# Joining 64-bit weights with a shift, equal halves of the query projection, and a list of the order written anew

## The chip, the cores and the metric

The kernel runs on one core of a Trainium2 chip. The metric is the device time of one execution in microseconds (us). The core's engines are named as in the profile: PE (TensorE) multiplies matrices, DVE (VectorE), ACT (ScalarE) and POOL (GpSimd) work element by element, and SP (SyncE) issues the transfers that the DMA engines carry out. SBUF is the core's working memory, PSUM the memory into which PE writes.

## The reference

A linear attention with exponential features feeds a feed-forward block with a squared ReLU:

```python
def phi(x):                      # x is q or k: (8, 8, 576, 64); w_phi: (64, 128)
    proj = np.einsum('bhsd,df->bhsf', x, w_phi)
    proj = proj - np.max(np.abs(proj), axis=-1, keepdims=True)
    return np.concatenate([np.exp(proj), np.exp(-proj)], axis=-1)
q_p, k_p = (phi(q), phi(k))
kv = np.einsum('bhsf,bhsd->bhfd', k_p, v)
z = np.sum(k_p, axis=2)
num = np.einsum('bhsf,bhfd->bhsd', q_p, kv)
den = np.einsum('bhsf,bhf->bhs', q_p, z)[..., None] + 1e-06
x = (num / den)                  # rearranged to (4608 tokens, 512)
h = x @ w_in                     # (512, 2048)
r = np.maximum(h, 0.0)
out = (r * r) @ w_out            # (2048, 512)
```

The two weight matrices arrive as 64-bit floats; q, k, v and w_phi are 32-bit.

## The kernel before

The attention works on 32 pairs of heads (8 batches of 8 heads). The first six pairs (`early`) get their denominators by extra matmuls; the other 26 (`late`, `visit`) do it by transposes and sums on DVE. In `visit` PE does the keys of one pair, the key-value product of the pair before and the numerators of the one before that, one behind another. In `late` the query projection (`q_proj`, L894) is done in four matmuls per pair: 512 columns for each of two heads into the PSUM tile pp, and the other 64 of each into pn and pv; three copies bring them to the SBUF tile pt, and POOL reduces pt over its partitions (L907).

The early pairs send their denominators through memory: a copy on ACT into sx, a DMA to den (L745), a reciprocal on DVE (L754, L755), a DMA to the scratch rd (L758) and one that spreads rd to rb (L765). DVE then multiplies the numerators n by rb (L772). The late pairs send the key-value block through a scratch too: td from kvs (L859), and eight transfers from td to kz (L864).

The feed-forward block takes 18 chunks of 256 tokens. A chunk has 8 steps, one for each slice of 256 hidden units. A step is a first product (`gemm1`, L973: 24 matmuls from the halves of the weights, win, and of the tokens, ring), then r, gh and ph on ACT and gl on DVE, and a second product (`gemm2`, L1000: 12 matmuls). The second product has three kinds of operands: gh with the high part wh, gh with the low part and gl with the near part. For slices 0 to 5 the low and near parts are bf16 tiles (wl); for slices 6 and 7 they are every second bf16 of float32r tiles (wout). Behind the last step of a chunk DVE scales the two PSUM banks po into the tile o, of which there is one buffer (L1011), and SP stores them (L1014).

Each of the 16 weight slices (8 of w_in, 8 of w_out, 1024 KB each) has to be joined from two 32-bit words to a 32-bit float. `prep` loads a slice into raw; ACT scales the high word into u (L435) and turns the low word into rounding bits (L440); DVE puts sign and rounding bits together (L443) and joins them with the shifted u (L447). A w_in slice then takes its maximum on ACT (L464); `power` spreads it over the partitions by a matmul (L389) and works out a scale on DVE (L393 to L397), and the scaled slice is split into win on ACT (L468) and DVE (L470). A w_out slice goes to its high part on ACT (L488), the low part on POOL (L300) and the near part on DVE (L495). Several slices lie in turn in the same SBUF space (home_of).

The order of all instructions is written by a planner. Every operation (`P.add`) has an engine, a duration, what it waits for and a rank; the planner runs a clock of its own and, on each engine, takes the ready operation of lowest rank. The ranks stand in a table of characters (RANKS). On the chip each engine and SP work strictly in the order so written.

Of the kernel before, what the change touches and what calls it, by code (L numbers as in the profile page):

```python
# [18 lines left out]
U32 = mybir.dt.uint32  # L19
AF = mybir.ActivationFunctionType  # L20
# [33 lines left out]
COLD = 1.15  # L54
# [9 lines left out]
class Op:  # L64
    __slots__ = ("n", "ways", "eng", "fn", "after", "uses", "rank", "land", "mode", "start", "end", "left", "next")

    def __init__(self, n, ways, after, uses, rank, land, mode):
        self.n, self.ways, self.rank, self.land, self.mode = n, ways, rank, land, mode
        self.take(next(iter(ways)))
        self.after, self.uses = [a for a in after if a is not None], list(uses)  # L70
        self.start = self.end = None

# [4 lines left out]
class Plan:  # L77
# [16 lines left out]
    def add(self, eng, us, fn, after=(), uses=(), rank=0.0, land=0.0, mode=WHOLE, lock=None, other=None):  # L94
        ways = {eng: (us, fn, lock)}
        if other:
            ways[other[0]] = other[1:]
        op = Op(len(self.ops), ways, after, uses, rank, land, mode if isinstance(mode, tuple) else (mode, mode))
        self.ops.append(op)
        return op  # L100

    def close(self):
# [6 lines left out]
        for (tag, n), mine in users.items():  # L109
            first = mine[0]  # L110
            if tag in self.single:
                if last := users.get((tag, (n[0], n[1] - 1))):
                    first.after += last[:1]
            else:
                if old := users.get((tag, n - self.bufs[tag])):
                    first.after += old
                if last := users.get((tag, n - 1)):
                    first.after.append(last[0])
            for op in mine[1:]:
                op.after.append(first)  # L120
# [28 lines left out]
    def order(self):  # L149
        for op in self.ops:  # L150
            op.start = op.end = None
            op.next, op.left = [], 0
            op.after = [a for a in {id(a): a for a in op.after}.values() if a is not op]
        for op in self.ops:
            for a in op.after:
# [6 lines left out]
        mode = WHOLE  # L162
# [6 lines left out]
        def release(op):  # L169
            least = max([open_at.get(tag, 0.0) for tag, n in alone(op)], default=0.0)  # L170
            for eng in op.ways:
                at = least
                for a in op.after:
                    at = max(at, a.end + a.land + (self.HOP[a.eng] if a.eng != eng or a.land else 0.0))
# [10 lines left out]
        while done < len(self.ops):  # L185
# [39 lines left out]
            free[e] = op.end  # L225
# [61 lines left out]
def tile_kernel(ctx, tc, qp, kp, vp, w_phi, w_in, w_out, out):  # L287
# [28 lines left out]
    wout = [None] * NFP  # L316
# [33 lines left out]
    td_ = tiles(dr, "td", [128, 256], F32, 2, EARLY)  # L350
    rb_ = tiles(at, "rb", [128, S], F32, 2)
    vm_ = tiles(sm, "vm", [128, NP], F32, 2)
    pw_ = tiles(sm, "pw", [128, 2], F32, 2)
# [11 lines left out]
    o_ = tiles(mp, "o", [128, DM], F32, 1)  # L365
# [9 lines left out]
    ld_w = P.add("SP", 1.5, lambda: SP.dma_start(wraw, w_phi), [], [], -100.0, land=2.0)  # L375
# [7 lines left out]
    def power(src, dst, top, after, uses, rank):  # L383
        n = power_n[0]
        power_n[0] += 1
        key = [("pw", n)] + uses

        def gather():
            PE.matmul(out=pn_["pw", n][:, 0:128], lhsT=src().to_broadcast([128, 128]), rhs=ident, start=True, stop=True)  # L389

        def bits():
            p = pw_[n]
            V.tensor_reduce(out=p[:, 0:1], in_=pn_["pw", n][:, 0:128], op=ALU.max, axis=AX.X)  # L393
            V.tensor_scalar(out=p[:, 1:2].bitcast(I32), in0=p[:, 0:1].bitcast(I32), scalar1=0x7F800000,
                            scalar2=None, op0=ALU.bitwise_and)
            V.tensor_scalar(out=dst[:, 0:1], in0=p[:, 1:2], scalar1=TINY, scalar2=top, op0=ALU.max, op1=ALU.mult)
            V.reciprocal(out=dst[:, 1:2], in_=dst[:, 0:1])  # L397

        a = P.add("PE", 0.3, gather, after, key + [("pn", ("pw", n))], rank)
        return P.add("DVE", 0.86, bits, [a], key + [("pn", ("pw", n))], rank)  # L400


# [9 lines left out]
    final = lambda f: f"h{f // 2} l{f // 2}".split() if f < NFP - 2 else [home_of[f, False]]  # L412

    def prep(n, f, of_in, rank):
# [3 lines left out]
        box = []  # L418
        raw = lambda: box[0]
        low_w, high_w = (lambda i=i: raw().rearrange("p (c w) -> p c w", w=2)[:, :, i] for i in range(2))  # L420
        u = lambda: u_[0][n]

        def load():
            box.append(cp.tile([128, 2048], I32, name=f"raw{f}{'io'[not of_in]}", tag=home))
            if of_in:
                SP.dma_start(raw().rearrange("p (t c) -> p t c", t=KT),
                             w_in[:, 512 * f:512 * f + 512].rearrange("(t p) c -> p t c", p=128))
            else:
                SP.dma_start(raw().rearrange("p (t c) -> p t c", t=2),
                             w_out[256 * f:256 * f + 256, :].rearrange("(t p) c -> p t c", p=128))  # L430

        def size():
            A.activation(out=u().bitcast(F32), in_=high_w().bitcast(F32), func=AF.Abs, scale=2.0 ** -111)  # L435

        def low():
            A.activation(out=low_w(), in_=low_w().bitcast(U32), func=AF.Copy, scale=0.875 * 2.0 ** -29, bias=0.4995)  # L440

        def ends():
            V.scalar_tensor_tensor(out=low_w(), in0=high_w(), scalar=word(0x80000000), in1=low_w(),  # L443
                                   op0=ALU.bitwise_and, op1=ALU.bitwise_or)
# [5 lines left out]
        def value(t):  # L450
            return u().bitcast(F32).rearrange("p (t c) -> p t c", t=t)

        ld = P.add("SP", 2.7, load, [home_read[home]] if home in home_read else [], [], rank - 3.0 + 0.3 * n, land=2.0)
        l = P.add("ACT", 1.14, low, [ld], [], rank)
        l = P.add("DVE", 1.22, ends, [l], [], rank, lock=4.0)
        o = P.add("ACT", 1.14, size, [ld], key, rank)
        o = P.add("DVE", 1.22, join, [o, l], key, rank, lock=4.0)
        if of_in:
            cs = slice(256 * f, 256 * f + 256)
            m = cw[:, f, :]  # L460
            pm = sm.tile([128, 1], F32, name=f"wm_{f}")

            def most():
                A.activation(out=raw()[:, 0:1024].bitcast(F32), in_=u().bitcast(F32), func=AF.Abs, accum_out=pm)  # L464

            o = home_read[home] = P.add("ACT", 1.06, most, [o], key, rank)
            o = power(lambda: pm, m, TOP_W, [o], [], rank)
            o = P.add("ACT", 1.1, lambda: A.activation(out=win[0][:, :, cs], in_=value(KT), func=AF.Copy, scale=m[:, 1:2]),  # L468
                      [o], key, rank)
            o = P.add("DVE", 1.5, lambda: V.scalar_tensor_tensor(  # L470
                out=win[1][:, :, cs], in0=value(KT), scalar=m[:, 1:2], in1=win[0][:, :, cs], op0=ALU.mult,
                op1=ALU.subtract), [o], key, rank, lock=4.0)
        else:
            home_read[home] = o
            j = slice(2 * (f % 2), 2 * (f % 2) + 2)

            def high():
                if f >= NFP - 2:
                    whole = cp.tile([128, 4, DM], F32R, name=f"wout{f}", tag=home)
                    wout[f] = whole[:, 0:2], whole[:, 2:4]  # L480
                else:
                    if f % 2 == 0:
                        both[f], both[f + 1] = [(
                            cp.tile([128, 4, DM], F32R, name=f"wh{f}", tag=final(f)[0]),
                            cp.tile([128, 8, DM], BF16, name=f"wl{f}", tag=final(f)[1]))] * 2
                    h, l = both[f]
                    wout[f] = h[:, j], l[:, j], l[:, slice(j.start + 4, j.stop + 4)]
                A.activation(out=wout[f][0], in_=value(2), func=AF.Copy)  # L488

            o = P.add("ACT", 1.1, high, [o] + [home_read[x] for x in final(f)], key, rank)  # L490
            last = [P.add("POOL", 2.5, lambda: sub(G, wout[f][1], value(2), wout[f][0].bitcast(F32)),
                          [o], key, rank, lock=0.0)]
            pool_prep.append(last[0])
            if f < NFP - 2:
                last.append(P.add("DVE", 0.75, lambda: V.tensor_copy(out=wout[f][2], in_=value(2)), [o], key, rank, lock=0.6,  # L495
                                  other=("ACT", 1.06, lambda: A.activation(out=wout[f][2], in_=value(2), func=AF.Copy), None)))
            return last
        return [o]

    both = {}  # L500
# [5 lines left out]
    def load_v(p, rank):  # L506
        v_load[p] = P.add("SP", 0.85, lambda: SP.dma_start(v_[p], vp[p]), [], [("v", p)], rank, land=2.0)
# [33 lines left out]
    def loads(p, rank):  # L541
        k_load[p] = P.add("SP", 0.75, lambda: SP.dma_start(k_[p], kp[p]), [], [("k", p)], rank, land=2.0)
# [577 lines left out]
```

## Time and profile before

| | us |
|---|---|
| median of 3 runs | 1072.16 |
| lowest, highest | 1069.67, 1072.84 |
| the profiled execution: its own time | 1070.77 |
| the profiled execution: span from the first to the last instruction | 1068.7 |

The profile's times count from the first instruction of one execution. The mean granted clock of PE was 0.989 of full speed. A busy engine is one on which an instruction was running; idle time is put down to what ended it.

### The profile page before, as it was taken

How to read it: one execution, taken by the hardware profiler on the slowest of the kernel's cores; microseconds unless marked ns; L12 is line 12 of the kernel's file. 1: busy time of each engine (PE TensorE's matmuls, PEld its weight loads, DVE VectorE, ACT ScalarE, POOL GpSimd, SP SyncE). 2: the span in 40 equal slices, each digit the busy share in tenths (PEclk: the TensorE clock that was granted, in tenths of full speed). 3: DMA queues.
4: the chain of work that ended last, by engine and by line, in shares of the span. 5: the costliest groups of instructions: out<-in, count | busy, mean ns of one | idle time of the engine just before them, and what ended most of it. 6: DMA issues, size and time to landing. Idle time of an engine off the chain costs nothing.

```text
span 1068.7 us, 19712 instructions
## 1 busy us (share of the span) xinstructions
PE 1037.3 (97%) x7762; PEld 706.9 (66%) x7762; DVE 740.5 (69%) x1561; ACT 635.1 (59%) x1129; POOL 135.3 (13%) x66
## 2 busy tenths in 40 slices
PE   7878999999999999999999999999999999999997
PEld 5545666676766666676666666666666666777774
DVE  6688898896879787778678768887887854112111
ACT  7888966756666565656455666656556545333232
POOL 0003122102020111111011111111110111000000
PEclk9898999999999999999999999999999999999999
DMA  9743322221222121212112112222121101000000
GB/s 348 257 147 102 132 82 70 72 66 49 70 72 63 44 60 52 76 57 76 57 44 72 46 48 56 77 56 77 44 63 24 51 13 41 1 20 20 2 20 20
DMA packets 68288, 73.48 MB, mean 69 GB/s; under 512 B 36836, under 2 KB 41828, under 8 KB 68196
## 3 DMA queue, kind: packets, MB, share of 16 engines
q1 hardware_dynamic: 68196, 72.23, 21.8%
q8 instruction: 61, 1.00, 0.4%
q14 instruction: 31, 0.25, 0.1%
HBM read 59.18 MB, written 12.99 MB: 68 GB/s over the span
## 4 chain that ended last, share of the span: by engine, by line
PE 86%; ACT 5%; DMA 4%; DVE 3%; SPq 2%; issue 1%; DVEq 0%; ACTq 0%
PE po L1000 35%; PE ph L973 33%; PE pv L606 4%; PE pp L550 2%; PE pn L824 2%; PE pp L894 2%; PE pv L824 2%; DMA den<-sx 1%; SPq L864 1%; PE pv L611 1%; PE pn L556 1%; DMA raw3i<-in_w_in_dram 1%; DMA out_dram<-o 1%; DMA k<-in_kp_dram 1%; DMA td<-kvs 1%
## 5 line engine op out<-in xcount | busy, mean ns | idle before, releaser
L973 PE MATMUL ph<-ring,win 128*128 128x256 f16 x3456 | 397.9, 273 | 1.3 <-DVE gl L300 1.3
L973 PEld LDWEIGHTS <-win 128*128 128x128 f16 x3456 | 335.8, 98 | 65.6 <-issue 5.5
L982 ACT ACTIVATE r<-ph,cw 128x512 f32<-128x512 f32 x144 | 98.8, 686 | 222.9 <-PE ph L973 222.3
L300 DVE TENSOR_TENSOR gl<-ph,gh 128x512 bf16<-128x512 f32 x144 | 98.9, 686 | 168.7 <-ACT ph L986 166.2
L907 POOL PARTITION_ALL_REDUCE mx<-pt x52 | 114.5, 2201 | 626.2 <-ACT pt L304 473.9
L1000 PE MATMUL po<-wh,gh 128*128 128x512 f32 x432 | 129.8, 421 | 2.6 <-DVE o L1011 2.5
L1000 PE MATMUL po<-wl,gh 128*128 128x512 bf16 x432 | 112.1, 382 | 0.0
L1000 PE MATMUL po<-wl,gl 128*128 128x512 bf16 x432 | 110.9, 379 | 0.0
L1000 PEld LDWEIGHTS <-gl 128*128 128x128 bf16 x576 | 56.1, 97 | 69.6
L984 ACT ACTIVATE gh<-r 128x512 fp32r<-128x512 f32 x144 | 90.7, 630 | 6.6 <-PE po L1000 2.3
L1000 PEld LDWEIGHTS <-gh 128*128 128x128 bf16 x576 | 44.8, 98 | 74.1 <-issue 39.5
L1000 PEld LDWEIGHTS po<-wh,gh 128*128 128x128 f32 x432 | 74.0, 189 | 22.3 <-issue 4.4
L986 ACT ACTIVATE ph<-r 128x512 f32<-128x512 f32 x144 | 84.1, 584 | 0.3
L1000 PE MATMUL po<-wout,gh 128*128 128x512 f32 (+1 forms) x288 | 76.1, 405 | 0.0
L606 PE MATMUL pv<-e,v 128*64 128x256 f32 x512 | 62.2, 386 | 0.0
L572 ACT ACTIVATE e<-e 128x512 f32<-128x512 f32 x64 | 39.8, 621 | 31.4 <-DVE e L569 31.2
L300 DVE TENSOR_TENSOR qe<-pt,mx 128x576 f32<-128x576 f32 x52 | 39.1, 753 | 26.9 <-POOL mx L907 26.7
L304 ACT ACTIVATE n<-pn 128x320 f32<-128x320 f32 (+1 forms) x32 | 13.8, 430 | 72.2 <-PE pn L824 70.1
L921 DVE SCALAR_TENSOR_TENSOR pt<-qe,zc,pt 128x576 f32<-128x576 f32 x52 | 41.9, 813 | 12.7 <-ACT pt L919 12.1
L912 ACT ACTIVATE qe<-qe 128x576 f32<-128x576 f32 x52 | 35.0, 673 | 25.1 <-DVE qe L300 25.1
L606 PEld LDWEIGHTS pv<-e,v 128*64 128x64 f32 x512 | 36.2, 140 | 16.4 <-issue 2.5
L1011 DVE TENSOR_SCALAR o<-po,cc 128x512 f32<-128x512 f32 x36 | 28.7, 798 | 25.4 <-DMA out_dram<-o 19.2
(207 smaller groups left out, 1380.1 us busy)
## 6 DMA issues: line engine op xcount, KB each, us to landing
v<-in_vp_dram SPq DMA_DIRECT2D x32, 320.0 KB
k<-in_kp_dram SPq DMA_DIRECT2D x32, 288.0 KB
q<-in_qp_dram SPq DMA_DIRECT2D x32, 288.0 KB
rb<-rd SPq DMA_DIRECT2D x64, 144.0 KB
out_dram<-o SPq DMA_DIRECT2D x36, 256.0 KB
td<-kvs SPq DMA_DIRECT2D x26, 128.0 KB
kz<-td SPq DMA_DIRECT2D x208, 16.0 KB
raw0i<-in_w_in_dram SPq DMA_DIRECT2D x1, 1024.0 KB
```

The source lines that it names most:

```text
L300: eng.tensor_tensor(out=out_, in0=a, in1=b_, op=ALU.subtract)
L572: o = P.add("ACT", act_us(512), lambda n=n: A.activation(out=e_[n][:, :, 1, :], in_=e_[n][:, :, 0, :], func=AF.Exp, scale=-1.0), [o], [("e ...
L606: PE.matmul(out=to[64 * h:64 * h + 64, 0:256], lhsT=v_[p][:, t, h, :], rhs=e_[2 * p + h][:, t].rearrange("p s f -> p (s f)"), start=t == 0 ...
L824: PE.matmul(out=to[64 * h:64 * h + 64, :], lhsT=kz_[n][:, 128 * s_ + 64 * h:128 * s_ + 64 * h + 64], rhs=qe_[2 * n + h].rearrange("p (s x) ...
L907: o = P.add("POOL", par_us(S), lambda n=n, h=h: G.partition_all_reduce(mx_[n], pt_[p][:, h, :], channels=128, reduce_op=bass_isa.ReduceOp. ...
L912: o = P.add("ACT", act_us(S), lambda qe=qe: A.activation(out=qe(1), in_=qe(0), func=AF.Exp, scale=-1.0), [o], [("qe", n)], R(RQ + 0.4))
L921: o = P.add("DVE", dve_us(S), lambda h=h, qe=qe, y=y: V.scalar_tensor_tensor(out=y(), in0=qe(1), scalar=zc_[p][:, 2 * h + 1:2 * h + 2], in ...
L973: PE.matmul(out=ph[:, j, :], lhsT=win[w][:, t, 128 * ff:128 * ff + 128], rhs=ring[half][x][:, t, c0:c0 + T], start=k == 0, stop=k == 3 * K ...
L982: o = P.add("ACT", act_us(512, 1), lambda: A.activation(out=r_[n], in_=ph_[bank], func=AF.Relu, scale=cw[:, f, 0:1]), [g1], [("ph", bank), ...
L984: sq = P.add("ACT", act_us(512), lambda: A.activation(out=gh_[n], in_=r_[n], func=AF.Square), [o], [("r", n), ("gh", n)], Q)
L986: o = P.add("ACT", 0.59, lambda: A.activation(out=ph_[bank], in_=r_[n], func=AF.Square), [o], [("ph", bank), ("r", n)], Q, other=("DVE", 0 ...
L1000: PE.matmul(out=po_[po[i][1]], lhsT=g[:, j, 128 * i:128 * i + 128], rhs=w[:, j, :], start=(ff == 0 and s == 0), stop=(ff == 2 * NFP - 1 an ...
```

## The change

- The DMA of a slice now reads rows that were laid out ahead: 8 KB for each partition, where before it read rows of 2 KB (w_in) or 4 KB (w_out).
- The join: the high word is scaled into u on ACT, or on DVE; ACT writes the rounding bits as one byte into the low byte of the high word; DVE shifts u by three bits (one input), and one two-input pass puts in sign and rounding bits. Before there were two two-input passes and no shift.
- Scales are worked out for two w_in slices at once: one chain of DVE operations for two matmuls.
- The high parts, the scaled slices and the low parts may be given to either of two engines by the planner. In the list as written 4 sizes, 1 high part and 1 scaled slice are on DVE, 2 of the near parts (those of slices 6 and 7, which are new) and none of the low parts left POOL.
- Slices 6 and 7 of w_out get the same tiles as the others (wh in float32r, wl in contiguous bf16).
- The query projection is two times 288 columns.
- Two buffers of o. The last chunk's scaling is done in halves, on DVE and ACT, each with a store of its own, and the very last second product finishes its first 128 tokens before it begins the others.
- The eight transfers from td to kz become four.
- The planner counts a transfer's time in the DMA queue (xfer) and several other durations anew, and RANKS is another table.

```diff
-    o_ = tiles(mp, "o", [128, DM], F32, 1)
+    o_ = tiles(mp, "o", [128, DM], F32, 2)
...
-            A.activation(out=u().bitcast(F32), in_=high_w().bitcast(F32), func=AF.Abs, scale=2.0 ** -111)
+        def size(E):
+            if E is A:
+                A.activation(out=u().bitcast(F32), in_=high_w().bitcast(F32), func=AF.Copy, scale=2.0 ** -111)
             else:
...
+                V.tensor_scalar(out=u().bitcast(F32), in0=high_w().bitcast(F32), scalar1=2.0 ** -111, scalar2=None,
+                                op0=ALU.mult)
 
         def low():
-            A.activation(out=low_w(), in_=low_w().bitcast(U32), func=AF.Copy, scale=0.875 * 2.0 ** -29, bias=0.4995)
-
-        def ends():
-            V.scalar_tensor_tensor(out=low_w(), in0=high_w(), scalar=word(0x80000000), in1=low_w(),
+            A.activation(out=low_byte(), in_=low_w().bitcast(U32), func=AF.Copy,
+                         scale=0.875 * 2.0 ** -29, bias=0.4995)
+
+        def shift():
+            V.tensor_scalar(out=u(), in0=u(), scalar1=3, scalar2=None, op0=ALU.logical_shift_left)
+
+        def join():
+            V.scalar_tensor_tensor(out=u(), in0=high_w(), scalar=word(0x80000007), in1=u(),
                                    op0=ALU.bitwise_and, op1=ALU.bitwise_or)
 
-        def join():
-            V.scalar_tensor_tensor(out=u(), in0=u(), scalar=3, in1=low_w(),
-                                   op0=ALU.logical_shift_left, op1=ALU.bitwise_or)
...
-            for lo, hi in ((0, 512), (512, S)):
+            for lo in (0, SH):
                 for h in range(2):
-                    PE.matmul(out=pp_["Q", p][:, h, :] if hi == 512 else tail(h), lhsT=wst[64 * h:64 * h + 64, :],
-                              rhs=q_[p][64 * h:64 * h + 64, lo:hi], start=True, stop=True)
...
+                    PE.matmul(out=rest(h) if lo else pp_["Q", p][:, h, 0:SH], lhsT=wst[64 * h:64 * h + 64, :],
+                              rhs=q_[p][64 * h:64 * h + 64, lo:lo + SH], start=True, stop=True)
...
-            low, near = wout[f][1:] if f < NFP - 2 else (upper(wout[f][1]), upper(wout[f][0]))
...
+            low, near = wout[f][1:]
+            parts = [(s, i) for s in range(3) for i in range(2)]
+            if n == NCH * NFP - 1:
+                parts = [(s, i) for i in range(2) for s in range(3)]
...
+        ways = ((V, slice(0, DM)),)
+        if c == NCH - 1:
+            ways = (V, slice(0, DM // 2)), (A, slice(DM // 2, DM))
```

Three places of the order. The first is SP's queue (the DMA queue) where the first two pairs' denominators set out (den from sx) and their reciprocals (rd from rc); raw are weight slices, and k, q, v loads of pairs. Before:

```order
L426 DMA raw2i<-in_w_in_dram 128x4x512
L745 DMA den_460<-sx_416 128x1x9
L507 DMA v_462<-in_vp_dram 128x640
L426 DMA raw5i<-in_w_in_dram 128x4x512
L758 DMA rd_510<-rc_495 128x9
L542 DMA k_513<-in_kp_dram 128x576
L426 DMA raw4i<-in_w_in_dram 128x4x512
L745 DMA den_549<-sx_541 128x1x9
```

And now:

```order
L543 DMA v_295<-in_vp_dram 128x640
L433 DMA raw0o<-in_w_out_dram 128x2048
L781 DMA den_384<-sx_380 128x1x9
L578 DMA k_397<-in_kp_dram 128x576
L579 DMA q_447<-in_qp_dram 128x576
L543 DMA v_462<-in_vp_dram 128x640
L794 DMA rd_538<-rc_532 128x9
L781 DMA den_542<-sx_536 128x1x9
```

Two weight slices that stood between the two trips now stand ahead of both; the loads ahead of the second trip are 9 slices, 7 v, 5 k and 4 q in both lists.

The second place is DVE where the first weight slice is joined (u), among the maxima (km, kmt, qm) and differences (e, et, pt) of the first pairs. Before:

```order
L443 SCALAR_TENSOR_TENSOR raw1i<-raw1i 128x1024
L579 TENSOR_TENSOR et_263<-pn_221,kmt_248 128x128
L569 TENSOR_TENSOR e_266<-po_174,km_210 128x4x128
L443 SCALAR_TENSOR_TENSOR raw0i<-raw0i 128x1024
L447 SCALAR_TENSOR_TENSOR u_212<-u_212,raw0i 128x1024
L678 TENSOR_REDUCE qm_306<-ph_272 128x4
```

And now:

```order
L460 TENSOR_SCALAR u_233<-u_233 128x1024
L612 TENSOR_REDUCE kmt_283<-pn_253 128x1
L463 SCALAR_TENSOR_TENSOR u_233<-raw0i,u_233 128x1024
L615 TENSOR_TENSOR et_299<-pn_253,kmt_283 128x128
L605 TENSOR_TENSOR e_301<-po_213,km_247 128x4x128
L460 TENSOR_SCALAR u_256<-u_256 128x1024
```

A two-input pass on raw has given way to a one-input shift of u ahead of the join.

The third place is PE at the very end, the second product of the last step; po are the two PSUM banks, one for each 128 tokens. Before:

```order
L1000 MATMUL po_11586<-wout_1692,gh_11834 128x512 x2
L1000 MATMUL po_11589<-wout_1692,gh_11834 128x512 x2
L1000 LDWEIGHTS gh_11834
L1000 MATMUL po_11586<-wout_1692,gh_11834 128x512
L1000 LDWEIGHTS gh_11834
L1000 MATMUL po_11586<-wout_1692,gh_11834 128x512
L1000 LDWEIGHTS gh_11834
L1000 MATMUL po_11589<-wout_1692,gh_11834 128x512
```

And now:

```order
L1039 MATMUL po_11426<-wh_1596,gh_11706 128x512 x2
L1039 LDWEIGHTS gh_11706
L1039 MATMUL po_11426<-wl_1706,gh_11706 128x512
L1039 LDWEIGHTS gh_11706
L1039 MATMUL po_11426<-wl_1706,gh_11706 128x512
L1039 LDWEIGHTS gl_11709
L1039 MATMUL po_11426<-wl_1706,gl_11709 128x512
L1039 LDWEIGHTS gl_11709
```

The first bank gets all of its six matmuls before the second gets any.

More of the change, by code (lines that the diff above doesn't have):

```diff
@@ L53 @@
 RA, RQ, RZ = 1.3, 0.4, 0.3
-COLD = 1.15
+COLD = 1.1
 def word(x):
@@ L71, in __init__ @@
         self.start = self.end = None
+        self.behind = []
     def take(self, eng):
@@ L117, in close @@
                 if last := users.get((tag, n - 1)):
-                    first.after.append(last[0])
+                    first.behind.append(last[0])
             for op in mine[1:]:
@@ L224, in order @@
                 mode = op.mode[1]
-            free[e] = op.end
+            free[e] = op.there = op.end
+            if op.land:
+                moved = max(moved, op.end) + op.xfer
+                op.there = moved + op.land
             done += 1
@@ L450, in value @@
[L450 to L497, printed above, removed]
@@ new lines, in out_low, with lower, near @@
+    def out_low(n, f, rank, high):
+        j = slice(2 * (f % 2), 2 * (f % 2) + 2)
+        at, key = [high, home_read[final(f)[1]]], [("u", n)]
+        def lower(E):
+            wout[f][1] = part(lows, f, BF16, "wl")[:, j]
+            sub(E, wout[f][1], value(n, 2), highs[f].bitcast(F32))
+        def near(E):
+            wout[f][2] = part(lows, f, BF16, "wl")[:, slice(j.start + 4, j.stop + 4)]
+            if E is A:
+                A.activation(out=wout[f][2], in_=value(n, 2), func=AF.Copy)
+            else:
+                V.tensor_copy(out=wout[f][2], in_=value(n, 2))
+        last = [P.add("POOL", 2.4, lambda: lower(G), at, key, rank, lock=0.0, other=("DVE", 1.23, lambda: lower(V), 4.0)),
+                P.add("DVE", 0.69, lambda: near(V), at, key, rank, lock=0.6, other=("ACT", 1.06, lambda: near(A), None))]
+        pool_prep.append(last[0])
+        return last + [high]
```

268 lines of the change are left out of this document (172 added, 96 removed).

## The prediction

> **What bounds the kernel now.** I read the page's busy times first, then the span cut into stages, then the list of what PE waited for.
>
> ```profile
> PE 1037.3 (97%) x7762; PEld 706.9 (66%) x7762; DVE 740.5 (69%) x1561; ACT 635.1 (59%) x1129; POOL 135.3 (13%) x66
> PEclk9898999999999999999999999999999999999999
> ```
>
> PE (TensorE) works 97% of the span, so the end can move in three ways only: less work on PE, less PE idle time, or fewer microseconds at a lower granted clock. The stages say where those are (columns: stretch, its length, then busy time and count of PE, weight loads, DVE, ACT, POOL, and at the end granted clock, DMA share and GB/s):
>
> ```profile
> 0.00:10.00 10.00, 4.31 (x36) 3.68 (x36) 4.11 (x12) 3.35 (x6) 0.68 (x6) 1.00 0.80 268
> 10.00:45.00 35.00, 30.31 (x388) 21.88 (x388) 26.37 (x52) 30.63 (x56) 2.36 (x1) 0.95 0.99 359
> 45.00:100.00 55.00, 44.62 (x434) 27.55 (x435) 44.70 (x84) 47.33 (x80) 4.95 (x2) 0.84 0.36 112
> 100.00:140.00 40.00, 38.23 (x287) 27.30 (x286) 35.50 (x49) 37.46 (x58) 8.84 (x4) 1.00 0.47 153
> 140.00:500.00 360.00, 360.00 (x2643) 244.09 (x2642) 298.40 (x658) 225.66 (x415) 58.48 (x28) 1.00 0.22 63
> 500.00:700.00 200.00, 197.50 (x1451) 134.11 (x1450) 152.11 (x337) 117.58 (x214) 29.17 (x13) 1.00 0.19 57
> 700.00:1062.00 362.00, 361.94 (x2530) 248.30 (x2529) 177.71 (x373) 173.14 (x304) 30.85 (x14) 1.00 0.11 32
> 1062.00:1068.70 6.70, 0.43 (x2) 0.00 (x0) 1.62 (x2) 0.00 (x0) 0.00 (x0) 0.79 0.20 78
> ```
>
> PE idles 5.7 us in the first ten, then 4.7, 10.4 and 1.8 us up to 140, nothing up to 500, 2.5 us between 500 and 700, and 6.3 us behind the last product. From 10 to 100 us the clock is also low: 30.3 x 0.05 + 44.6 x 0.16 = 8.7 us. So 140 to 1062 is a pure PE bound, where each microsecond of PE work removed comes off the end and work moved among ACT, DVE and DMA is worth nothing. The head (10 to 140) is where the preparation of the weights competes with the first pairs on ACT (115.4 busy of 130 us) and DVE (106.6); up to 45 us the DMA engines are full as well (0.99). The waits of PE, in us in all, times, longest:
>
> ```profile
> PE po L550 <- DVE e L569: 3.0, 1, 3.0
> PE pp L667 <- ACT qe L712: 2.8, 1, 2.8
> PE pv L651 <- DVE kvs L305: 2.5, 1, 2.5
> PE po L1000 <- DVE o L1011: 2.5, 2, 1.6
> PE pn L720 <- DVE pw L393: 1.6, 1, 1.6
> PE ph L973 <- DVE gl L300: 1.3, 1, 1.3
> ```
>
> All but the o row lie in the head: there PE follows DVE and ACT.
>
> **Second product of slices 6 and 7: -2.9 us.** Their low and near operands were every second bf16 of float32r tiles (wout); they become contiguous bf16 like the others. One step of each kind:
>
> ```profile
> 966.44 1.18 PE L1000 MATMUL po<-wh,gh 128*128 128x512 f32 x4
> 967.45 1.04 PE L1000 MATMUL po<-wl,gh 128*128 128x512 bf16 x4
> 969.19 2.78 PE L973 MATMUL ph<-ring,win 128*128 128x256 f16 x24
> 971.73 2.09 PE L1000 MATMUL po<-wout,gh 128*128 128x512 f32 x8
> 974.56 0.27 PE L973 MATMUL ph<-ring,win 128*128 128x256 f16 x1
> ```
>
> From first start to the next product it is 969.19 - 966.44 = 2.75 us with wl and 974.56 - 971.73 = 2.83 us with wout. 36 such steps (2 slices, 18 chunks) by 0.08 is 2.9 us, all on PE. Slice 6 now gets its low parts only after slice 7 is joined; that is hidden only if slice 7 is ready by the first chunk's seventh step, and a delay there counts in the head.
>
> **Query projection in equal halves: -2.9 us.** Instead of 512 and 64 columns, 288 and 288, in 26 pairs. The second fence shows the nearest four matmuls of 288 columns (two at a time on halves of the array, as here).
>
> ```profile
> 257.77 1.13 PE L894 MATMUL pp<-q,wraw 64*128 64x512 f32 x4
> 258.73 0.22 PE L894 MATMUL pn<-q,wraw 64*128 64x64 f32 x1
> 259.00 0.50 PE L1000 MATMUL po<-wh,gh 128*128 128x512 f32 x1
> ...
> 145.24 1.19 PE L720 MATMUL pn<-qe,kz 128*64 128x288 f32 x8
> 146.36 2.79 PE L973 MATMUL ph<-ring,win 128*128 128x256 f16 x24
> ```
>
> Before: 0.96 us for 512 columns and 0.27 for 64, 1.23 in all. By columns alone 64 would need 0.12; so the short matmuls are held by something of fixed cost. 288-column matmuls take 146.36 - 145.24 = 1.12 us. Saving 0.11 x 26 = 2.9; ends: 0 (nothing gained) and 0.15 x 26 = 3.9 (the whole excess of the short ones). I take 2.9, since that row has the same width, type and concurrency. The three copies to SBUF keep 1152 columns in sum and hide beside PE.
>
> **Two output buffers: -2.5 us.** The o row above is the whole idle time of 140 to 1062 but 0.06. The second of two scalings had to wait for the first one's store; with two buffers it follows at once. Ends: 0 if another wait stands there, 2.5. I take 2.5. The new list no longer puts two first products in a row at the ends of the last chunks; there one of them (2.54 us, 971.73 - 969.19) must cover two scalings of 0.81 (next fence), which it does with 0.9 us to spare.
>
> **The tail: -2.8 us.** The last second product finishes its first 128 tokens before the rest, and each block is scaled as two halves, on DVE and ACT, with stores of their own.
>
> ```profile
> 1062.02 0.81 DVE L1011 TENSOR_SCALAR o<-po,cc 128x512 f32<-128x512 f32 x1 [2.48 <-PE po L1000]
> 1064.98 0.81 DVE L1011 TENSOR_SCALAR o<-po,cc 128x512 f32<-128x512 f32 x1 [2.15 <-DMA out_dram<-o]
> ...
> 1062.86 3.30 SPq L1014 DMA_DIRECT2D out_dram<-o  x2
> ```
>
> Now the second store is issued at about 1065.8 and the span ends 2.9 us later. Half a scaling costs between half of 0.81 and all of it; I take the middle, 0.6. Then the last halves are ready at 1062.6, one issue of 0.35 (1066.16, the end of the two issues, less 1065.8) stands before the last, and the span ends 2.9 us after 1063.0: 1065.9 for 1068.7.
>
> **The preparation of 16 slices.** One row for each kind of operation (duration: mean; for L495 and L393 min/median/max):
>
> ```profile
> L443 DVE SCALAR_TENSOR_TENSOR raw0i<-raw0i 128x1024 int32<-128x1024 int32 x1 | 1.2, 1229 | 0.0
> L435 ACT ACTIVATE u<-raw4i 128x1024 f32<-128x1024 f32 x1 | 1.2, 1152 | 0.0
> L495 DVE CAST wl<-u x6: 632/690/2857, 44.6 to 124.0; 128x1024 bf16<-128x1024 f32 x6
> L393 DVE TENSOR_REDUCE pw<-pn x16: 240/285/292, 30.6 to 747.7; 128x1 f32<-128x128 f32 x16
> L488 ACT ACTIVATE wh<-u 128x1024 fp32r<-128x1024 f32 x6 | 6.3, 1054 | 0.0
> L468 ACT ACTIVATE win<-u,cw 128x1024 f16<-128x1024 f32 x8 | 9.2, 1148 | 0.0
> ```
>
> Off DVE go 16 two-input passes, 16 x 1.23 = 19.7 us. On it come 16 shifts, 4 sizes, 1 high part and 1 scaled slice. No integer shift stands in the trace; it is bounded by the one-input CAST (0.69) and the two-input L443 (1.23), and I take 0.69, because it has one input of 1024 words, as the CAST has. 22 x 0.69 = 15.2. Four scale chains fewer, each L393 (0.29) and three tiny operations of about 0.15: -3.0. DVE: -7.5. ACT loses 4 sizes (1.15), one high part (1.05) and one scaled slice (1.15), and takes 2 near parts (1.05, as L488): -4.7. The rounding now writes one byte in eight instead of a word in eight; between 0 and 16 x 1.15 dearer, and I take 0, its reads being unchanged. The maximum, the join and POOL's 8 subtractions stay.
>
> What of this reaches the end? Counting each engine's instructions in the two lists at durations like these, the new one has asked ACT and DVE for about 4 us less by the eighth step of the first chunk, while PE's work up to there is equal. ACT is busy 86% of 45 to 100, so 4 us come out of that stage's 10.4 idle, and with them about a quarter (2 us) of the clock loss. Head: -6. Upper end: half of idle and clock loss of 10 to 140 (16.9 + 8.7), -13. Lower end: +2, because the scratch trip of the denominators still stands behind weight loads:
>
> ```profile
> 37.88 6.36 DMA den<-sx
> ...
> 44.26 0.17 DVE L754 TENSOR_SCALAR den<-den 128x9 f32<-128x9 f32 x1 [4.26 <-DMA den<-sx]
> ```
>
> That trip cost DVE 4.3 us and PE the 3.0 of row L569. Both lists issue the same 14.4 MB before it (9 weight slices, 7 v, 5 k, 4 q); no work saved on DVE makes those bytes pass sooner, and by the same count DVE reaches the row after 2 us less work. The weights' rows become 8 KB each, at the same bytes: 0. Half the DMA issues of kz (104 for 208) shorten a trip on which PE never waited: 0.
>
> **Sum.** 2.9 + 2.9 + 2.5 + 2.8 + 6 = 17.1 off the profiled execution's 1070.8 (its span of 1068.7 and 2.1 around it, which stays): 1053.7, say 1054. That execution is 1.4 us under the median of the three runs, 1072.2; I leave that inside the range.
>
> **Rivals.**
> - The head gives nothing: DMA to 45 us and the denominators' trips set it. 1070.8 - 11.1 = 1059.7. For it: 0.99 DMA share; against it: 17.5 of the 25.6 us lost lie at 45 to 100, where DMA is at 0.36.
> - The head gives 13 us: 1046.6. For it: that same stage.
> - POOL holds DVE. A CAST that met POOL's subtraction:
>
> ```profile
> 101.57 3.16 POOL L300 TENSOR_TENSOR wl<-u,wh 128x1024 bf16<-128x1024 f32 x1 [3.55 <-ACT wh L488]
> ...
> 102.43 2.86 DVE wl L495
> ```
>
> It took 2.86 instead of 0.69 and ended 0.6 us after POOL; PE's 1.3 us wait for gl follows. Two of six CASTs were so stretched. If the 22 new one-input passes meet the other 6 subtractions, DVE loses 6 x 2.2 = 13 us, of which its idle time at 45 to 140 (14.8) takes about half: the head gives nothing and loses 1 more, 1061. The Trainium skill, "SBUF — State Buffer", section "SBUF: two separate sides", says the pair of ports that DVE and GpSimd share is locked for a whole instruction and the loser fully blocks; the 2.86 us agree. By that rule the shifts are exposed, but the removed passes, with two SBUF inputs, were too, so it speaks for few extra meetings.
> - Slower: the trips stop DVE in front of every den row. One of six stopped it now; should the other five stop it for a full 6.36, PE behind it, 32 us come on top: 1054 + 32 = 1086. It decides from four such stops, since 1070.8 + 3.2 is 20.3 above the sum. Against it: the later pairs' trips run while DMA is at 0.36.
> - The halves gain nothing on PE: 1056.5, inside the range.
>
> **Chances.** The sum 0.50 (1049 to 1058); head gives nothing 0.18; head gives 13 us 0.17; POOL 0.09; trips 0.06. Range 1044 to 1065: it spans the sum, both ends of the head and POOL. A difference of 0.3% (3.2 us) is about what measurement can tell from none. All but the trips lie faster; some of the weak cases could fall within 0.3%: faster 0.87, same 0.07, slower 0.06.
>
> **What would show it.** After: second products of slices 6 and 7 of 2.75 us; a query projection of about 1.12 us from its start to the next row; no PE wait for o; the last store under 1.2 us after the last scaling's start; shifts near 0.69 us; a PE idle time from 10 to 140 near 13 us. I am wrong if shifts take 1.2, if den rows stop DVE more than once, or if PE idles anew after 140.

## The result and the profile after

| | us |
|---|---|
| before, median of 5 runs beside it | 1070.79 |
| after, median of 5 runs (lowest, highest) | 1077.13 (1075.32, 1078.00) |
| ratio, with its 95% interval | 1.0053 (1.0036 to 1.0071) |
| profiled execution after: span | 1076.2 (before 1068.7) |

The changed kernel is 0.5% slower. The forecast was 1054, 1044 to 1065. The busy times and the granted clock of the kernel after:

```profile
PE 1038.8 (97%) x7762; PEld 711.0 (66%) x7762; DVE 730.6 (68%) x1546; ACT 655.2 (61%) x1133; POOL 137.0 (13%) x66
PEclk9897899999999999999999999999999999999999
```

DVE lost 9.9 us of work, as the change meant; ACT gained 20.1 where the prediction took 4.7 off. The stages of the kernel after, in the columns of the prediction's table (stretch, length, busy time and count of PE, weight loads, DVE, ACT, POOL, then granted clock, DMA share, GB/s):

```profile
10.00:45.00 35.00, 25.69 (x278) 19.32 (x280) 18.67 (x43) 28.95 (x53) 0.00 (x0) 0.93 0.85 343
45.00:100.00 55.00, 42.97 (x455) 25.94 (x453) 47.45 (x78) 52.00 (x79) 7.37 (x3) 0.87 0.37 112
100.00:140.00 40.00, 35.16 (x287) 23.75 (x285) 29.28 (x46) 35.60 (x46) 7.92 (x3) 0.90 0.36 128
140.00:500.00 360.00, 357.65 (x2637) 245.45 (x2638) 292.05 (x642) 235.36 (x416) 59.59 (x26) 1.00 0.21 63
500.00:700.00 200.00, 200.00 (x1455) 136.61 (x1452) 158.28 (x352) 123.76 (x228) 30.36 (x14) 1.00 0.22 63
```

From 10 to 140 us PE now idles 26.2 us (9.3, 12.0, 4.8) where it idled 16.9, and 2.35 more behind 140; ACT is busy for 52.0 of the 55 us from 45 to 100. The lower clock costs 25.69 x 0.07 + 42.97 x 0.13 + 35.16 x 0.10 = 10.9 us where it cost 8.7. Behind 500 PE is never idle: the wait for o is gone. What PE waited for (us in all, times, longest):

```profile
PE pv L687 <- ACT kvs L310: 9.1, 5, 5.1
PE pp L737 <- ACT qe L748: 5.1, 3, 3.8
PE pn L773 <- ACT n L310: 4.2, 2, 4.0
...
PE pn L709 <- ACT sx L310: 2.4, 1, 2.4
```

Four rows on ACT stand where before ACT and DVE shared them. ACT's new work is in one line. Of the two rows, the first is one of 16 like it in the kernel after, the second the shift (group, count, busy time, mean ns of one, idle time ahead):

```profile
L456 ACT ACTIVATE raw0i<-raw0i 128x1024 uint8<-128x1024 uint32 x1 | 2.5, 2540 | 0.0
L460 DVE TENSOR_SCALAR u<-u 128x1024 int32<-128x1024 int32 x16 | 10.9, 683 | 2.1 <-ACT u L450 2.0
```

The 16 writes of the rounding bytes take 2.48 to 2.61 us each. In the kernel before the same line wrote words, in 1.11 to 1.23 (mean 1.15), so 16 x 1.37 = 22 us were added to ACT, all of them ahead of 164 us. Who waited for these writes is in the trace, too:

```profile
  DVE u L463: 11.6, 12
```

12 of the 16 joins on DVE stood still for them, 11.6 us in all.

### The profile page after: what moved, and what is told of

Its sections match the earlier page's. It is cut to its first block, busy times and chain, and to the rows that moved or that the text cites. A ratio compares the mean times of both kernels' runs of the same rounds, so it can differ in the third digit from the quotient of the medians.

```text
span 1076.2 us, 19519 instructions
## 1 busy us (share of the span) xinstructions
PE 1038.8 (97%) x7762; PEld 711.0 (66%) x7762; DVE 730.6 (68%) x1546; ACT 655.2 (61%) x1133; POOL 137.0 (13%) x66
## 4 chain that ended last, share of the span: by engine, by line
PE 88%; ACT 8%; DMA 2%; DVE 1%; issue 1%; SPq 0%; ACTq 0%
PE po L1039 35%; PE ph L1009 35%; PE pv L642 4%; PE pn L860 3%; PE pp L586 2%; PE pv L860 2%; PE pp L930 2%; PE pn L930 1%; PE pv L647 1%; ACT u L450 1%; PE pn L592 1%; DMA den<-sx 1%; DMA raw7i<-in_w_in_dram 1%; DMA v<-in_vp_dram 1%; ACT sx L549 0%
## 5 line engine op out<-in xcount | busy, mean ns | idle before, releaser
L1009 PE MATMUL ph<-ring,win 128*128 128x256 f16 x3456 | 402.7, 274 | 0.0
L1039 PE MATMUL po<-wh,gh 128*128 128x512 f32 x576 | 171.5, 419 | 0.0
L1039 PE MATMUL po<-wl,gh 128*128 128x512 bf16 x576 | 149.6, 382 | 0.0
L1039 PE MATMUL po<-wl,gl 128*128 128x512 bf16 x576 | 148.0, 379 | 0.0
L1039 PEld LDWEIGHTS po<-wh,gh 128*128 128x128 f32 x576 | 98.4, 189 | 28.5 <-issue 9.1
L955 ACT ACTIVATE pt<-qe,zc 128x576 f32<-128x576 f32 x52 | 40.2, 773 | 5.6 <-DVE zc L921 1.3
L894 DVE STREAM_TRANSPOSE kvs<-pv 128x256 f32<-128x256 f32 x26 | 11.6, 447 | 45.7 <-PE pv L860 44.1
```

Of the source, the lines that this page charges most:

```text
L955: o = P.add("ACT", act_us(S, 1), lambda h=h, qe=qe, y=y: A.activation(out=y(), in_=qe(0), func=AF.Copy, scale=zc_[p][:, 2 * h:2 * h + 1]), ...
L1009: PE.matmul(out=ph[:, j, :], lhsT=win[w][:, t, 128 * ff:128 * ff + 128], rhs=ring[half][x][:, t, c0:c0 + T], start=k == 0, stop=k == 3 * K ...
L1039: PE.matmul(out=po_[po[i][1]], lhsT=g[:, j, 128 * i:128 * i + 128], rhs=w[:, j, :], start=(ff == 0 and s == 0), stop=(ff == 2 * NFP - 1 an ...
```

## The experiments

In all comparisons the kernel before ran on the same chip; ratios are to it. Theory A (in the expectations of the first four) holds that the byte writes on ACT make the kernel slower, B that the new list does, C that any write narrower than a word is dear. "The same lists" means that every engine has the same instructions in the same order.

**1. Two bytes in place of one** (after, the same lists)

```diff
-    box[0].bitcast(U8)[:, 4:8192:8]
+    box[0].bitcast(U16)[:, 2:4096:4]
```

> The changed kernel with one edit: ACT writes the rounding bits as 16-bit instead of 8-bit integers, into the low half of the same high word; same values, same order on every engine. Theory A (the byte write): one such activation falls from 2.52 us to about 1.15, 16 x 1.37 = 22 us leave ACT in the head, PE follows, and the time falls by 15 to 22 us, to 1055 to 1062. Theory B (the new list is worse in itself, its scratch trips and new waits, and the longer activations sit in ACT's slack): it stays within 5 us of the changed kernel, 1072 to 1077, whatever the activation takes. Theory C (writes narrower than a word are slow at any width): the activation stays near 2.5 us and the time at 1077.

Ratio 1.0036 (1.0021 to 1.0050), 1076.8 us: as after, so A's forecast for this run was a miss and C's came true. One of the 16 rows:

```profile
L457 ACT ACTIVATE raw0o<-raw0o 128x1024 uint16<-128x1024 uint32 x1 | 2.5, 2534 | 0.0
```

Sixteen bits at a step of 8 bytes are as dear as eight.

**2. A word in place of the byte** (after, the same lists)

```diff
-    box[0].bitcast(U8)[:, 4:8192:8]
+    box[0][:, 0:2048:2]
```

> The changed kernel with the rounding bits written as 32-bit integers over the low word, where the join does not read them: the rounding of the weights is left out. Same order, same number of passes. Theory A: as with 16 bits, 1055 to 1062, the activation near 1.15 us. Theory B: 1072 to 1077. Theory C: 1055 to 1062 here, but 1077 with 16 bits.

Ratio 0.9899 (0.9885 to 0.9914), 1061.4 us: 15.7 below after by the medians, 16.5 by the ratios. The write, at the same step of 8 bytes:

```profile
L456 ACT ACTIVATE raw0o<-raw0o 128x1024 int32<-128x1024 uint32 x1 | 1.2, 1188 | 0.0
```

So the byte writes cost about 16 of the 22 us that they add to ACT, and B falls for that part: with the same list the kernel beats the one before. The join does not read this word, so the weights stay unrounded here and in experiments 5, 6, 7 and 10; 8, 9, 11 and 12 compute all values.

**3. The byte writes alone** (before, the same lists)

```diff
-            A.activation(out=low_w(), in_=low_w().bitcast(U32), func=AF.Copy, ...
+            A.activation(out=raw().bitcast(U8)[:, 4:8192:8], in_=low_w().bitcast(U32), func=AF.Copy, ...
...
-            V.scalar_tensor_tensor(out=low_w(), in0=high_w(), scalar=word(0x80000000), in1=low_w(),
-                                   op0=ALU.bitwise_and, op1=ALU.bitwise_or)
+            V.scalar_tensor_tensor(out=low_w(), in0=high_w(), scalar=word(0x80000007), in1=high_w(),
+                                   op0=ALU.bitwise_and, op1=ALU.bitwise_and)
```

> The kernel before with one edit: ACT writes the rounding bits as bytes into the low byte of the high word (a stride of 8 bytes), and the first two-input pass reads that word for them. Where ACT reads the high word only afterwards, the last bits of the weights are wrong. Same order. Theory A: 16 x 1.37 = 22 us more on ACT, which was busy in 86% of the stage from 45 to 100 us: 12 to 22 us slower, 1083 to 1093. Theory B: ACT has room, within 4 us of 1071.

Ratio 1.0096 (1.0081 to 1.0111), 1082.5 us, 10 above before; the writes take 2.47 to 2.57 us here. The direction is A's; the size is under A's 12 to 22. That ACT had more room in that list would explain it, but isn't shown.

**4. Four forms of the write** (after, the same lists, a single execution)

```diff
-    box[0].bitcast(U8)[:, 4:8192:8]
+    (box[0].bitcast(U8)[:, 4:8192:8], box[0].bitcast(U8)[:, 0:2048:2],
+     box[0].bitcast(U8)[:, 0:1024], box[0].bitcast(U16)[:, 0:1024])[n % 4]
```

> The changed kernel with four forms of the rounding write, four slices each: bytes 8 bytes apart, bytes 2 apart, bytes side by side, 16-bit integers side by side. The weights come out wrong; only the durations count. If the byte as such is dear, the first three take 2.5 us and the last 1.15; if the step between bytes is what costs, the first takes 2.5, the second less, and the third 1.15.

One row of each form, in the order of the diff (all have four):

```profile
L458 ACT ACTIVATE raw1o<-raw1o 128x1024 uint8<-128x1024 uint32 x1 | 2.5, 2508 | 0.0
...
L458 ACT ACTIVATE raw1i<-raw1i 128x1024 uint8<-128x1024 uint32 x1 | 1.2, 1177 | 0.0
...
L458 ACT ACTIVATE raw0o<-raw0o 128x1024 uint8<-128x1024 uint32 x1 | 1.2, 1155 | 0.0
...
L458 ACT ACTIVATE raw7o<-raw7o 128x1024 uint16<-128x1024 uint32 x1 | 1.2, 1162 | 0.0
```

Bytes that lie 2 apart or side by side, and 16 bits side by side, take 1.11 to 1.23 us, like words. C falls in its plain form: it is neither the byte nor the step, but the two together.

**What experiment 2 left open.** Its 1061.4 is 11.1 below before, and the terms on PE's own path (below) are 9.5; so the head had gained 1 to 2 us, not 6. The trace of experiment 2 shows what ate the rest (start, duration, instruction, idle time ahead and what ended it):

```profile
38.07 0.74 ACT L549 ACTIVATE sx<-v 128x640 bf16<-128x640 f32 x1 [8.21 <-DMA den<-sx]
...
40.41 0.90 PE L687 MATMUL pv<-ident,kvs 128*128 128x128 f32 x3 [7.76 <-ACT kvs L310]
```

L549 takes the absolute values of v for their maximum and throws them into sx. The same sx holds the denominators that the DMA to den reads, and in the chain of work (start, duration) that DMA, which stands behind weight loads in the queue, fills 11.29 us:

```profile
26.70 11.29 DMA den<-sx
```

So ACT stopped for 8.2 us over a scratch tile, and PE behind it for 7.8. The kernel after has the same wait, of 5.49 us. The kernel before had one of this kind, but a small one (start, duration, as above):

```profile
80.17 0.74 ACT L513 ACTIVATE sx<-v 128x640 bf16<-128x640 f32 x1 [1.30 <-DMA den<-sx]
```

Two things differ in the new order. The first den DMA stands behind 9 weight slices where it stood behind 7: issued at 29.7 us it landed at 38.2, before it was issued at 30.0 and DVE read its data at 34.5. And ACT's next write to sx is now an absolute value of v, where before it was the second pair's denominators. Theory H: this wait costs what the head should have gained; W: the weights' work would end the head there anyway.

**5. A scratch tile of its own** (experiment 2, the same lists)

```diff
-                out=sx_["va", p].bitcast(BF16)[:, 0:640], in_=v_[p]...
+                out=sv, in_=v_[p]...
```

> The kernel after with the low word's rounding left out as in e2_word (ACT writes its codes as 32-bit words), and the absolute values of v written to a scratch tile of their own instead of the tile that den's DMA reads; the lists are e2_word's. e2_word was 1061.4 on a chip where the kernel before was 1072.5. Theory H (what the head should have gained is lost because ACT's absolute values of v wait 8.2 us for the first den DMA, which stands behind the weights): that wait goes, PE's wait of 7.8 us for kvs shrinks by as much, and the time is 5 to 8 us below e2_word, about 1055. Rival W (the weights' own work on ACT and DVE ends the head whenever that wait does): within 2 us of e2_word.

Ratio 0.9829 (0.9812 to 0.9845), 1053.9 us: 7.5 under experiment 2 by the ratios. Stages of experiment 2 and of 5, from 10 to 45 us:

```profile
10.00:45.00 35.00, 24.98 (x278) 18.99 (x280) 18.13 (x43) 26.11 (x51) 0.00 (x0) 0.82 0.84 341
```

```profile
10.00:45.00 35.00, 31.74 (x387) 22.75 (x389) 26.71 (x60) 33.15 (x65) 0.01 (x1) 1.00 0.92 363
```

PE idles 3.3 us where it idled 10.0, and its clock is granted in full where 0.82 had cost another 24.98 x 0.18 = 4.5 us: with the wait went clock, too. Some of both comes back from 45 to 100, where 5 idles 12.0 us and 2 idles 9.4. H holds, W falls.

**6 and 7. Three weight loads behind the den DMA** (experiment 2, and experiment 5; SP's order alone is another)

```diff
+        behind(w_load[0, False], v_load[NP + 2])
+        behind(w_load[5, True], den_trip[1])
+        behind(w_load[3, True], den_trip[1])
```

> e2_word with three weight loads moved in SyncE's order: slice 0 of the output half behind the load of v of pair 6, slices 5 and 3 of the first half behind the den DMA of pair 1; the same scratch tile. The low word's rounding is left out as in e2_word. Theory H: the den DMA starts about 3 MB of loads earlier, the wait on it falls from 8.2 us to under 2, time 5 to 8 us below e2_word (1054 to 1056). Theory W, or the moved slices come late themselves: 1060 to 1064.

> The scratch tile of e5 and the moved loads of e6 together, the low word's rounding left out. Theory H: not more than 2 us below the better of e5 and e6, since both take away one wait (1053 to 1056). If the den DMA and the scratch tile were two separate losses: 1048 to 1050. Theory W: 1060 to 1063.

Ratios 0.9885 (0.9870 to 0.9900) and 0.9867 (0.9853 to 0.9882), 1059.8 and 1057.7 us. The first isn't to be told from experiment 2, the second is 4 us above 5; H's forecasts, 1054 to 1056 and 1053 to 1056, were misses. In both ACT takes the absolute values of v without a wait, at 31 us; but PE has a wait that wasn't there, here in 6:

```profile
PE pn L759 <- DVE et L618: 3.9, 1, 3.9
```

It goes back to the same trip. Two of the moved loads (raw3i, raw5i) now stand in the queue ahead of its last transfer, which spreads rd to rb. In 6 that transfer fills 7.29 us of the chain of work, from 42.49 on, and DVE waits for it ahead of et:

```profile
DVE rb L812 <- DMA rb<-rd: 3.8, 1, 3.8
```

In 5 the same wait is 0.62 us, in 7 it is 4.57. The move took these loads from in front of the trip's first transfer and put them in front of its last.

**8. The four parts on PE's path, in the kernel before**

```diff
-    o_ = tiles(mp, "o", [128, DM], F32, 1)
+    o_ = tiles(mp, "o", [128, DM], F32, 2)
...
-            for lo, hi in ((0, 512), (512, S)):
+            for lo in (0, SH):
...
-            low, near = wout[f][1:] if f < NFP - 2 else (upper(wout[f][1]), upper(wout[f][0]))
+            low, near = wout[f][1:]
...
+        if c == NCH - 1:
+            ways = (V, slice(0, DM // 2)), (A, slice(DM // 2, DM))
```

> The kernel before with only four parts of the change: equal halves of the query projection, two output buffers, the second low product of slices 6 and 7 from a bfloat16 tile, the last stage by halves. The weights' preparation stays as it was, all values are computed. If these four are worth what their places in the traces show (2.9 + 1.3 + 2.5 + 3.0 = 9.7 us, all on PE's path) and the head is left as it was: 1072.5 - 9.7 = 1062.8, a ratio of 0.991. By the terms as they were predicted (2.9 + 2.9 + 2.5 + 2.8 = 11.1): 1061.4. If the two more casts on DVE and the new list cost PE something in the head: 1065 to 1070.

Ratio 1.0107 (1.0088 to 1.0126), 1083.4 us: every forecast was missed, by 13 us or more. The edit, with two more casts on DVE for slices 6 and 7, made the planner write the list anew, and the new list has three waits behind 160 us that the kernel before has not:

```profile
PE pp L582 <- DVE e L601: 4.8, 1, 4.8
PE pp L926 <- DVE e L601: 4.5, 1, 4.5
PE pn L856 <- ACT qe L946: 4.1, 1, 4.1
```

The stretches with these waits have less clock as well:

```profile
200.00:240.00 40.00, 34.87 (x256) 23.18 (x256) 36.55 (x84) 24.21 (x48) 4.32 (x2) 0.96 0.26 73
...
320.00:340.00 20.00, 15.47 (x106) 9.71 (x106) 16.48 (x34) 10.19 (x20) 3.06 (x2) 0.88 0.28 83
340.00:380.00 40.00, 35.69 (x260) 25.00 (x260) 34.20 (x71) 24.01 (x44) 8.28 (x4) 0.93 0.19 47
```

13.4 us of waits and 34.87 x 0.04 + 15.47 x 0.12 + 35.69 x 0.07 = 5.8 of clock are 19.2; with them the 1062.6 that the four parts should give (1072.1 - 9.5) becomes 1081.8, under 2 us below what was measured. The run doesn't show what the parts are worth alone; it shows that a new list is a term of its own, here about twice as large as all the parts together.

**9. The scratch tile in the kernel after** (the byte writes stay, the same lists; all values computed). The edit is that of 5.

> The kernel after, with its byte writes, and the scratch tile of e5 for the absolute values of v; the lists are those of after, all values are computed. Theory H: the two losses are separate, the wait of ACT (5.5 us in after) for den's DMA goes and the time falls by 4 to 8 us, to 1069 to 1073 where after was 1077. Rival S: with 22 us more on ACT the byte writes alone end the head, the wait lay beside them, and the time is within 2 us of 1077.

Ratio 0.9971 (0.9962 to 0.9981), 1068.9 us: 8.8 below after by the ratios, a little more than H's 4 to 8, and S falls. The two losses are separate: by the ratios the byte writes cost 16.5 us with the shared tile (after against 2) and 0.9971 - 0.9829 = 1.42%, 15 us, without it (9 against 5).

**10. Two parts undone** (experiment 5, the same lists)

```diff
+    o_.n = 1
...
-            for lo in (0, SH):
+            for lo, hi in ((0, 512), (512, S)):
```

> e5_split (ratio 0.983 to the kernel before) with two parts of the change undone under the same lists: one output buffer, and the query projection in pieces of 512 and 64 columns. The low word's rounding is left out as in e5. By the places measured in the traces: 2.5 us for the buffer and 26 x 0.05 = 1.3 us for the projection, together 3.8, a ratio of 0.9865. By the terms as predicted (2.5 and 2.9): 5.4, 0.988. If neither lies on PE's path: 0.983.

Ratio 0.9974 (0.9963 to 0.9985), 1068.9 us: 1.45% or 15.5 us above 5, where 3.8 to 5.4 were expected. The projection gave its part: from its start to the next instruction it takes 1.23 us in all 25 of 160 to 900 us, and 1.17 in experiment 5. The buffer gave far more:

```profile
PE po L1041 <- DVE o L1059: 10.5, 11, 2.6
```

PE waited 11 times for o, 10.5 us, where the kernel before with its one buffer waited twice, 2.5. DVE's scalings waited 18 times for a store here, 42.7 us, in the kernel before 6 times, 19.2. The kernel before had a list written for one buffer; a list written for two needs two. 10.5 + 26 x 0.06 = 12.1 of the 12.8 us between the two profiled spans.

**11 and 12. All values, without most byte writes.** Both start from 5. In 11 the lists stay: for the 12 slices whose size is on ACT, the rounding is a word over the low word again, and DVE joins by the two passes of the kernel before, in the places of shift and join. In 12 all 16 slices do so and the planner writes the lists anew.

```diff
+            if swapped:
+                V.scalar_tensor_tensor(out=low_w(), in0=high_w(), scalar=word(0x80000000), in1=low_w(),
+                                       op0=ALU.bitwise_and, op1=ALU.bitwise_or)
...
+                V.scalar_tensor_tensor(out=u(), in0=u(), scalar=3, in1=low_w(),
+                                       op0=ALU.logical_shift_left, op1=ALU.bitwise_or)
```

> e5_split with every value computed again: for the 12 slices whose sizes stand on ACT, ACT writes the codes as 32-bit words over the low words and DVE joins them by the two two-input passes of the kernel before, in the places that the lists have for the shift and the join; the other 4 slices keep the byte write. Against e5 DVE does 12 x 0.54 = 6.5 us more and ACT 4 x 1.37 = 5.5 us more in the first 140 us. Theory: these lie partly beside other work, so 0 to 10 us above e5, 1054 to 1064, a ratio of 0.984 to 0.992. If DVE's passes and not ACT's writes set the head: 1066 or more.

> The same arithmetic as e11 for all 16 slices, the two passes given to the planner with their real durations, so that it makes the lists anew. Theory: the planner places DVE's longer passes at least as well as lists made for shorter ones: equal to e11 or up to 4 us less. Rival L (a new list can lose as much as a part of the change gains, as e8 did by three new waits of 13.4 us behind 160 us): 1065 to 1085.

Experiment 11: ratio 0.9881 (0.9865 to 0.9896), 1058.7 us, as expected, and faster than before and after. DVE is busy for 51.15 us of 45 to 100 instead of 45.51, and the ratio stands 0.52%, 5.6 us, above experiment 5; against experiment 9, which has the byte writes in these 12 slices, it is 10 us below. Experiment 12: ratio 1.0086 (1.0072 to 1.0100), 1080.7 us, for the same arithmetic. Its list has new waits, here its stretch from 160 to 500, which has no idle time in 11:

```profile
160.00:500.00 340.00, 331.35 (x2401) 225.64 (x2401) 267.52 (x600) 206.40 (x378) 54.39 (x25) 0.98 0.20 58
```

8.65 us idle, and 331 x 0.02 = 6.6 of clock. Rival L held; the forecast that the planner would do no worse was a miss.

## Why the prediction was wrong, point by point

**The step that failed** is in the head: "The rounding now writes one byte in eight instead of a word in eight; between 0 and 16 x 1.15 dearer, and I take 0, its reads being unchanged." It measured 16 x 1.37 = 22 us, beyond its own upper end of 18.4, and on ACT, the engine which the prediction itself had at 86% of 45 to 100. Only the reads were looked at; the write was what changed. And the upper end didn't go into the range: 16 x 1.15 on an engine that PE follows would have put the kernel back at 1072. Experiment 2 against after, and 5 against 9, show 15 to 16.5 us of it at the end.

**The head, -6**, was right only without two losses. With words alone (experiment 2) it gave 1 to 2; with the scratch tile too (5) it gave 1072.1 - 1053.9 = 18.2 less the 9.5 of the other terms, so 8.7. (The profiled execution of 5 was its slowest; between the profiled spans, 1068.7 - 1055.2, the head gives 4.) That experiment 5 measured the forecast sum of 1054 is luck: it leaves out the rounding and has a scratch tile that the change has not. The ACT wait over sx is the second omission: the prediction named the den DMA behind the weight loads and charged it to DVE (its 4.26 us row), and never asked who else writes the tile that the DMA reads. It also counted the loads ahead of the second trip alone, where both lists have 9 slices; the trip on which ACT waited is the first, with 9 for 7.

**The second product of slices 6 and 7**, -2.9, was right. A step of the kernel after:

```profile
971.68 1.18 PE L1039 MATMUL po<-wh,gh 128*128 128x512 f32 x4
...
974.43 0.82 PE L1009 MATMUL ph<-ring,win 128*128 128x256 f16 x6
```

974.43 - 971.68 = 2.75 us, and each of the eight steps from 940 to 980 us takes 2.75 or 2.76, slices 6 and 7 among them.

**The query projection**, -2.9, was mis-sized; it is -1.5:

```profile
308.76 0.76 PE L930 MATMUL pp<-q,wraw 64*128 64x288 f32 x4
...
309.94 1.20 PE L1039 MATMUL po<-wh,gh 128*128 128x512 f32 x4
```

1.17 to 1.18 us, not the 1.12 of the numerators' row that had the same width; 26 x 0.06 = 1.5. It lies inside the ends of 0 and 3.9.

**Two output buffers**, -2.5, was right for the kernel before: no row of PE waits for o any more, and 500 to 700 is full. Under the new list a single buffer costs PE 10.5 (experiment 10).

**The tail**, -2.8, was about right: behind the last product PE idled 6.3 us and now 3.7, so -2.6, with a wait that wasn't foreseen: ACT's half begins after DVE's half of the same block, not beside it.

```profile
1072.54 0.54 DVE L1057 TENSOR_SCALAR o<-po,cc 128x256 f32<-128x256 f32 x1 [0.79 <-PE po L1039]
1073.11 0.47 ACT L1059 ACTIVATE o<-po,cc 128x256 f32<-128x256 f32 x1 [0.86 <-DVE o L1057]
```

**The shifts**, 0.69, measured 0.683, and none was held by POOL the way that the 2.86 us CAST had been: the longest of the 16 took 0.694. The other new one-input passes took at most 0.75. Three other instructions were held, each begun while a subtraction of POOL ran:

```profile
80.08 2.93 DVE L808 TENSOR_TENSOR rb<-n,rb 128x576 f32<-128x576 f32 x1
90.43 2.19 DVE L404 TENSOR_SCALAR pw<-pw 128x2 int32<-128x2 int32 x1
121.18 3.27 DVE L532 SCALAR_TENSOR_TENSOR win<-u,cw,win 128x1024 f16<-128x1024 f32 x1
```

Others of their lines take 0.75, 0.17 and 1.28 us, so DVE lost 6.2; in the kernel before the two CASTs had cost it 4.2 up to 140. The 13 us that the POOL rival feared didn't come. Neither did stops of DVE at the den rows (DVE waits for den nowhere). "PE idles anew after 140" came, 2.35 us: a wait of 1.91 for DVE's et, which was behind a join that had stood still 1.49 for a byte write, and one of 0.45 for ACT's maximum of the same slice.

**The account of the result.** Off PE's path went 2.9 + 1.5 + 2.5 + 2.6 = 9.5 us. The head lost 26.2 - 16.9 = 9.3 of idle time, 10.9 - 8.7 = 2.2 of clock, and 2.35 idle with 17.65 x 0.09 = 1.6 of clock (granted at 0.91) from 140 to 160, less 0.5 in the first ten: 15. That makes +5.5 of the 7.5 between the spans; 2.0 us of the profiled execution have no place here. PE's idle time is all accounted for, so they lie in its busy time or in the estimate of the clock's cost.

## What to carry to other kernels

When an instruction's output changes its type or its step, price the write by a row that writes like that; if there is none, the cost is unknown, and its upper end belongs into the range with the engine's share of busy time beside it. Of a DMA that comes late, ask not only who reads what it brings but who must write next what it still reads: a scratch tile that is written only to be thrown away needs no neighbour. And an edit that makes a planner write a new order brings a term of its own: here two new lists cost some 20 us each, and in experiment 12 for arithmetic that under the other list (11) was faster than before.

## What the hardware showed that was not expected

- An ACT write of 1024 elements per partition at a step of 8 bytes takes 2.47 to 2.61 us with 8 bits and 2.48 to 2.60 with 16, but 1.11 to 1.23 with 32; 8 bits 2 bytes apart or side by side and 16 bits side by side take 1.11 to 1.23 as well. Steps of 4 bytes weren't tried, nor the same writes on DVE or POOL, and why it is so isn't shown.
- PE's lost clock went along with its idle time, but not by its amount alone. In the 35 us from 10 to 45 the clock was granted in full with 3.3 us idle (experiment 5) and at 0.82 with 10.0 (experiment 2), but at 0.93 with 9.3 (after), and with 4.7 us idle at 0.95 (before) and in full (experiment 8).
